# Loading a quarter of one weight piece by transfers of 8 partitions, on DMA engines 0 to 7 alone

## The chip, the cores and the metric

One core of one Trainium2 chip. The metric is the device time of one execution in microseconds, median of several.

## The reference

Two branches work on the same layer-normalised row block of four rows (batch 4, one position, D = 576), and their outputs are summed with the input: attention over the last 2048 positions of a cache (16 key/value heads, 32 query heads of 128), and a mixer with a gated MLP.

```
xn = layernorm(x)
h  = gelu(layernorm(xn) @ w1); hs = shift(h) @ w2; x1 = xn + hs
h2 = gelu(layernorm(x1) @ w3) @ w4            # w3: 576 x 4608, w4: 4608 x 576
out = x + attention(xn, k_cache, v_cache, wq, wo) + (x1 + h2)
```

The arithmetic is small. The weights and the cache windows, 88.5 MB in bfloat16, have to be read once.

## The kernel before

(A partition is one of the 128 rows of the on-chip memory, SBUF. A DMA engine is one of 16 units that move data between memories. A semaphore is a counter that engines raise and wait for.)

Every engine has a list of operations with sort keys; all loads but one small one are issued from one queue (SyncE), in the order wq, w2, w1, w3, K cache, V cache with wo in between, and w4 last. w4 comes in five pieces of 18, 9, 6, 2 and 1 rows per partition, so that little matmul work remains after the last one:

```python
W4_ROWS = (18, 9, 6, 2, 1)
...
for n, rc in enumerate(W4_ROWS):
    v = w4_t[:, len(w4tile) * D:(len(w4tile) + rc) * D]
    ev_w4.append(add_dma([(v, B_w4[base:base + 128 * rc, :].rearrange("(p r) n -> p (r n)", r=rc))], ("w4", n),
                         ["hT1", "hs1"] if n == 0 else [], KT + 5 + n))
    # ... (tiles of the piece are noted, base advances)
```

`add_dma` issues one transfer for each pair of destination and source and counts 16 semaphore increments for each. TensorE waits for a piece and accumulates it:

```python
for n, (t0, t1_) in enumerate(W4N):
    # f: for each tile t of the piece and each half h: ACC[h] += h2T[:, t]^T @ w4 tile
    if n < last_p:
        add("pe", f, waits=[ev_w4[n]], sig=f"MO{n}", key=KT + 20 + n)
    # else: one operation for each half, so that both halves can be copied and stored at once
```

A piece of `rc` rows is a transfer of 128 partitions with one contiguous run of `rc` x 1,152 bytes each: 20,736, 10,368, 6,912, 2,304 and 1,152 bytes. A tile `kt` of 32 KB per partition (transposed keys, then probabilities) is free after the middle of the kernel; the experiments use it as a target for additional loads.

## Time and profile before

| | before |
|---|---|
| median time | 216.02 us (215.91 to 217.14, 6 runs) |
| span of the profiled execution | 214.1 us |
| read from memory | 88.49 MB, 427 GB/s from 20 to 208 us |
| last landing of w4 | 211.47 us |

The page is read here by three things: the row of DMA share in the slices (which engine is full), the chain that ended last (what the end hangs on), and the stretches near the end. The prediction below shows these lines. Two more things come from the trace's own records rather than from a view: the time of each semaphore increment (16 for a transfer of 128 partitions, which I read as one for each DMA engine that finishes its part), and the start and duration of each packet. A packet here is one contiguous run: 10,368 bytes take 389 ns on one engine, 6,912 take 262, 2,304 take 93.

These are the one-microsecond stretches of the kernel before near its end. The columns are the stretch and its length, busy time of PE, PEld, DVE, ACT and POOL, the granted clock, the DMA share and GB/s:

```profile
206.00:207.00 1.00, 1.00 (x20) 0.72 (x18) 0.00 (x0) 0.00 (x0) 0.00 (x0) 1.00 0.92 387
207.00:208.00 1.00, 1.00 (x14) 0.48 (x10) 0.00 (x0) 0.00 (x0) 0.00 (x0) 1.00 1.02 430
208.00:209.00 1.00, 1.00 (x9) 0.36 (x8) 0.00 (x0) 0.00 (x0) 0.00 (x0) 1.00 0.98 400
209.00:210.00 1.00, 1.00 (x18) 0.55 (x14) 0.00 (x0) 0.00 (x0) 0.00 (x0) 1.00 0.76 289
210.00:211.00 1.00, 0.62 (x12) 0.41 (x12) 0.00 (x0) 0.00 (x0) 0.00 (x0) 1.00 0.44 165
```

The rate stays near 400 until 209 us and then falls with the DMA share: engines run out of work, those that still work keep their pace (289 GB/s at a share of 0.76, 165 at 0.44; packets of 2,304 bytes take 93 ns before 209 us and after). In such short stretches a long packet seems to be counted whole in one of them (a share goes up to 1.22 below), so a value may be off by some tens of GB/s.

### The profile page before, as it was taken

The numbers are of one execution on the slowest core, as the hardware profiler recorded it, in microseconds if no ns is written. First come the engines' busy times: TensorE is split into PE (matmuls) and PEld (weight loads), VectorE is DVE, ScalarE is ACT, GpSimd is POOL, SyncE is SP. The second block draws the span as 40 slices with busy tenths as digits, with TensorE's granted clock in tenths as the row PEclk, the third lists the DMA queues.
The fourth block names the chain that finished last, engine by engine and source line by source line (L and its number), as shares of the span: only waits on it lengthen the run. The fifth ranks groups of instructions, "written<-read, shape, count | busy, mean of one in ns | idle before, by whom it ended". The sixth has DMA issues, their size and how long they took to land. (4 is left out here: it accounts for less than half of the span.)

```text
span 214.1 us, 5906 instructions
## 1 busy us (share of the span) xinstructions
PE 145.6 (68%) x2642; PEld 108.9 (51%) x2646; DVE 76.5 (36%) x150; ACT 61.0 (29%) x75; POOL 10.9 (5%) x37
## 2 busy tenths in 40 slices
PE   0157787999999999999996178033444333336995
PEld 0023312888878887888774068033434333334542
DVE  5305400577676676666664830100010011001000
ACT  2001402466655665666666620000000000000000
POOL 8301000000001000000000000000000000000000
PEclk9999699999999999999999655555555555555799
DMA  7999999999999999999999999999999999999992
GB/s 282 404 385 445 441 407 438 419 427 416 435 429 429 422 435 429 424 426 435 429 426 426 429 429 425 419 432 429 429 422 429 435 429 419 430 436 426 428 409 104
DMA packets 7459, 88.66 MB, mean 414 GB/s; under 512 B 1292, under 2 KB 1688, under 8 KB 2456
## 3 DMA queue, kind: packets, MB, share of 16 engines
q1 hardware_dynamic: 7432, 88.50, 97.7%
q8 instruction: 8, 0.13, 0.2%
q14 instruction: 3, 0.02, 0.0%
q10 hardware_dynamic: 16, 0.01, 0.0%
HBM read 88.49 MB, written 0.00 MB: 413 GB/s over the span
## 5 line engine op out<-in xcount | busy, mean ns | idle before, releaser
L340 PE MATMUL ps<-perm_bf,ring 128*128 128x128 bf16 x1024 | 61.7, 220 | 0.6
L340 PEld LDWEIGHTS ps<-perm_bf,ring 128*128 128x128 bf16 x1024 | 57.5, 98 | 8.9 <-issue 8.6
L347 DVE COPY kt<-ps 128x1024 bf16<-128x1024 bf16 x80 | 52.3, 687 | 24.8 <-PE ps L340 24.3
L421 PE MATMUL ps<-PTpad,ring 128*128 128x8 bf16 x1024 | 29.7, 168 | 41.2 <-PEq L584 37.7
L346 ACT ACTIVATE kt<-ps 128x1024 bf16<-128x1024 bf16 x48 | 48.5, 1023 | 29.1 <-PE ps L340 28.3
L421 PEld LDWEIGHTS ps<-PTpad,ring 128*128 128x128 bf16 x1024 | 28.7, 104 | 42.3 <-issue 42.2
L561 ACT ACTIVATE out_sb<-ps 4x288 bf16<-4x288 f32 x1 | 0.4, 401 | 87.2 <-PE ps L438 87.2
L354 PE MATMUL ps<-kt,Qs 128*32 128x512 bf16 x272 | 17.8, 382 | 1.4 <-PEq L584 1.4
L410 DVE TENSOR_TENSOR PTpad<-PT,mU_bf 128x512 bf16<-128x512 bf16 x16 | 6.4, 420 | 29.7 <-PE ps L421 29.7
L433 DVE TENSOR_TENSOR OTn<-ps,rinvB 128x32 bf16<-128x32 f32 x4 | 0.8, 191 | 34.2 <-PE ps L421 34.2
L523 PE MATMUL ps<-w,x1nT 128*32 128x384 bf16 (+2 forms) x65 | 11.3, 766 | 0.8 <-DMA w<-in_B_w_dram 0.5
L354 PEld LDWEIGHTS ps<-kt,Qs 128*32 128x32 bf16 x272 | 5.8, 96 | 6.8 <-issue 1.5
L375 POOL COPY Qs<-Qpad 128x128 bf16<-128x128 bf16 x16 | 4.6, 293 | 87.0 <-PE ps L354 75.0
L301 PE MATMUL ps<-kt,xnT 128*32 128x512 bf16 x32 | 3.6, 631 | 4.3 <-DMA kt<-in_A_wq_dram 4.3
L523 PEld LDWEIGHTS ps<-w,x1nT 128*32 128x32 bf16 x65 | 3.3, 113 | 6.3 <-issue 3.9
L438 PE MATMUL ps<-w,ORT 128*4 128x288 bf16 x64 | 5.8, 357 | 0.4 <-DVE ORT L460 0.4
L278 PE MATMUL ps<-ident_bf,xn_bf 4*128 4x4 bf16 x8 | 0.6, 170 | 8.0 <-DVE ragsrc L271 8.0
L560 DVE CAST out_sb<-ps 4x288 bf16<-4x288 f32 x1 | 0.4, 446 | 14.5 <-PE ps L438 14.5
L438 PE MATMUL ps<-w,h2T_sb 128*4 128x288 bf16 x72 | 5.0, 286 | 0.4 <-DMA w<-in_B_w_dram 0.4
L392 PE MATMUL ps<-kt,permT_bf 128*128 128x512 bf16 x3 | 1.8, 608 | 4.9 <-DVE kt L391 4.8
L544 DVE COPY h2T_sb<-ps 128x16 bf16<-128x16 bf16 x1 | 0.2, 166 | 13.6 <-PE ps L538 13.6
L438 PEld LDWEIGHTS ps<-w,ORT 128*4 128x4 bf16 x64 | 3.3, 106 | 3.1 <-DVE ORT L460 1.0
(99 smaller groups left out, 61.6 us busy)
## 6 DMA issues: line engine op xcount, KB each, us to landing
ring<-in_A_k_cache_dram SPq DMA_DIRECT2D x32, 1024.0 KB, 13.0
ring<-in_A_v_cache_dram SPq DMA_DIRECT2D x32, 1024.0 KB, 15.1
w<-in_B_w_dram SPq DMA_DIRECT2D x2, 2304.0 KB, 22.9
w<-in_A_wo_dram SPq DMA_DIRECT2D x2, 2304.0 KB, 20.3
kt<-in_A_wq_dram SPq DMA_DIRECT2D x1, 4096.0 KB, 12.2
w<-in_B_w_dram SPq DMA_DIRECT2D x1, 2592.0 KB, 27.4
w<-in_B_w_dram SPq DMA_DIRECT2D x3, 576.0 KB, 14.5
w<-in_B_w_dram SPq DMA_DIRECT2D x1, 1296.0 KB, 30.0
```

The lines of the kernel that those rows point to most:

```text
L301: ins = e.matmul(Qps[k][32 * g:32 * g + 32, :], lhsT=x_, rhs=w, start=(r == 0), stop=(r == 4), tile_position=(0, 32 * g), skip_group_check ...
L340: ins = e.transpose(tb[n % 4][:, t, :], slot_t(c)[:, 8 * k + t, :], perm_bf[:])
L346: return "act", lambda e: e.activation(out=ktbuf[:, n % 16], in_=tb[n % 4], func=ACTF.Copy)
L347: return "dve", lambda e: e.tensor_copy(out=ktbuf[:, n % 16], in_=tb[n % 4])
L354: ins = e.matmul(Sps[32 * u:32 * u + 32, q, :].rearrange("p (t i) -> p t i", t=16), lhsT=Qs[:, c % NPOS, 32 * u:32 * u + 32], rhs=ktgrp[:, ...
L375: P(lambda e, c=c, cc=cc: e.tensor_copy(out=Qs[:, c % NPOS, :], in_=Qpad_t[:, 128 * cc:128 * cc + 128]), waits=["qT", "qs_zero"] + ([f"SC{ ...
L392: add("pe", lambda e, q=q: e.matmul(ps[:, 4 + q % 3, :], lhsT=permT_bf[:], rhs=PTx[:, q, :], start=True, stop=True), waits=[f"PTx{q}", "pe ...
L410: return lambda e: e.tensor_tensor(out=PTpad[:, c % 2], in0=PTv[:, :, cc, :].unsqueeze(2).to_broadcast([128, NT, NU, 2]), in1=mU_bf[:].uns ...
L421: ins = e.matmul(o_, lhsT=slot_t(c)[:, t, :], rhs=PTpad[:, c % 2, t].rearrange("p u e -> p (u e)"), start=(t == 0), stop=(t == NT - 1))
L433: add("dve", lambda e, hv=hv: e.tensor_tensor(out=hv(OTn), in0=OTps.rearrange("p (b h) -> p b h", b=B), in1=hv(rinvB), op=ALU.mult), waits ...
L438: return e.matmul(ACC[h], lhsT=lhsT, rhs=rhs, start=start, stop=stop, tile_position=(0, 32 * h), skip_group_check=True)
L523: ins = e.matmul(H2ps[k][32 * g:32 * g + 32, 128 * off:128 * (off + cnt)].rearrange("p (c x) -> p c x", c=cnt), lhsT=x_, rhs=w.rearrange(" ...
```

## The change

At the end eight of the 16 DMA engines finish after the other eight. The change is meant to shift a little work: of the second piece, three quarters of the partitions (p mod 4 = 0, 1, 2) are loaded by transfers of 32 partitions, which all 16 engines share, and the last quarter (p mod 4 = 3) by four transfers of 8 partitions, which engines 0 to 7 carry alone. Engines 0 to 7 then carry 10 rows of this piece and engines 8 to 15 carry 6, instead of 8 each.

The packet records carry no engine number, so these numbers are names: 0 to 7 are the eight engines that carry a transfer of 8 partitions.

```diff
+LOW8 = 1
 W4_ROWS = (18, 9, 6, 2, 1)
...
             v = w4_t[:, len(w4tile) * D:(len(w4tile) + rc) * D]
-            ev_w4.append(add_dma([(v, B_w4[base:base + 128 * rc, :].rearrange("(p r) n -> p (r n)", r=rc))], ("w4", n),
+            w4_src = B_w4[base:base + 128 * rc, :].rearrange("(p r) n -> p (r n)", r=rc)
+            rows = [slice(0, 128)] if n != LOW8 else [slice(a, 128, 4) for a in range(3)] + [slice(3 + a, 32 + a, 4) for a in range(0, 128, 32)]
+            ev_w4.append(add_dma([(v[a], w4_src[a]) for a in rows], ("w4", n),
                                  ["hT1", "hs1"] if n == 0 else [], KT + 5 + n))
```

## The prediction

> **What bounds the kernel now.** I began with the slices of the page: if one row is full over the whole span, that row is the bound.
>
> ```profile
> PE   0157787999999999999996178033444333336995
> DMA  7999999999999999999999999999999999999992
> GB/s 282 404 385 445 441 407 438 419 427 416 435 429 429 422 435 429 424 426 435 429 426 426 429 429 425 419 432 429 429 422 429 435 429 419 430 436 426 428 409 104
> ...
> HBM read 88.49 MB, written 0.00 MB: 413 GB/s over the span
> ```
>
> DMA is the only row at 9 from the second slice to the last but one; PE sits at 3 or 4 for a third of the span. The kernel is a stream of 88.49 MB at some 427 GB/s, and no compute engine sets its time. The chain that ended last says where the end hangs:
>
> ```profile
> by line: DMA w<-in_B_w_dram 14.6%; SPq L177 1.2%; PE ps L421 0.9%; PE ps L438 0.6%; issue 0.3%; DVE out_sb L560 0.2%
> ...
> 179.19 31.22 DMA w<-in_B_w_dram
> 210.41 0.04 issue
> 210.46 1.39 PE ps L438 x18
> 211.85 0.44 DVE out_sb L560
> ```
>
> From 179 to 210 us the end waits for w4, then for 18 short matmuls, a cast and the store. The timeline of the end shows that PE follows each piece as it lands:
>
> ```profile
> 205.32 2.37 PE L438 MATMUL ps<-w,h2T_sb 128*4 128x288 bf16 x36
> 207.62 1.25 PE L444 MATMUL ps<-zeros_bf 128*128 128x512 bf16 x5
> 208.81 1.27 PE L438 MATMUL ps<-w,h2T_sb 128*4 128x288 bf16 x18
> 210.46 1.35 PE L438 MATMUL ps<-w,h2T_sb 128*4 128x288 bf16 x18 [0.38 <-DMA w<-in_B_w_dram]
> 211.51 0.08 PEld L438 LDWEIGHTS ps<-w,h2T_sb 128*4 128x4 bf16 x2 [0.23 <-DMA w<-in_B_w_dram]
> ```
>
> The last line is the key: the last weight loads still wait 0.23 us for a DMA, so the last landing sets the end. After it come about 2.6 us of fixed tail. Stretches show that the DMA engines do not all stop together:
>
> ```profile
> 20.00:208.00 188.00, 135.54 (x2533) 104.19 (x2538) 69.46 (x128) 58.36 (x70) 3.81 (x13) 0.77 1.01 427
> 208.00:212.00 4.00, 3.42 (x41) 1.57 (x38) 0.16 (x1) 0.13 (x1) 0.00 (x0) 1.00 0.54 214
> ```
>
> The last two columns are DMA share and GB/s. Before 208 us the 16 engines are full; afterwards only part of them works.
>
> The trace's semaphore records give each engine's landing. The 16 increments of the last w4 piece come at 209.54 to 210.45 us (eight), then, after a gap, at 210.97 to 211.47 (eight). Early on the spread is small: 24.03 to 24.46 us for the second piece of w3. So eight engines are late at the end, and the kernel ends with the latest of them. Why they are late: another queue carries a few big packets.
>
> ```profile
> q8 instruction: 8, 0.13, 0.2%
> ```
>
> Each has 16,384 bytes and takes 1.01 to 1.10 us. Packet records carry no engine number, but a packet starts about 4 ns before the end of the one before it on its engine, so I chained them into 16 lanes. Seven lanes stall once by 1.00 to 1.08 us, each at the end of one of the first seven such packets (27.4, 41.5, 49.6, 118.7, 127.6, 133.9, 159.1 us); an eighth lane is late by about as much from 47 us on, without a record that explains it. These eight lanes are the late ones. The eighth packet, at 209.0 us, meets the lane that had led.
>
> [...]
>
> **The change part by part.** The second piece has 128 rows of 10,368 bytes (1,296 KB), 8 rows per engine, median 389 ns a packet: 3.11 us per engine.
> - *Moved:* three transfers of 32 partitions give every engine 3 x 2 = 6 rows. Four transfers of 8 partitions give engines 0 to 7 four more. So 0 to 7 carry 10 rows and 8 to 15 carry 6: plus and minus 2 x 0.389 = 0.78 us. Bytes are unchanged.
> - *Added in the stream:* one semaphore packet per transfer and engine. One costs about 10 ns between data packets, and the next packet 5 ns (267 against 262 ns). Engines 0 to 7 have six more, about 0.09 us; 8 to 15 two more, 0.03 us.
> - *Added on the issuing queue:* six more issues at about 0.44 us (median of the w rows) put the last issue near 183 us instead of 180.5. Nothing of w4 lands before 197 us: hidden.
> - *PE, DVE, ACT:* the instruction order is the same. The piece's wait moves to a full count of 112.
>
> If 8 to 15 are the late ones, the late group's last landing goes from 211.47 to 211.47 - 0.78 + 0.03 = 210.72, the early group's from 210.45 to 210.45 + 0.78 + 0.09 = 211.32. The maximum falls by 0.15 us. PE keeps up: the third piece lands by about 210.25 instead of 210.41, so the matmuls ahead of the last also move up. On 215.94 this gives 215.79, and I say **215.8 us**. The means favour this reading: the groups lie about 1.2 us apart, and the change moves 1.56 us of difference between them, so it overshoots somewhat. More could not be gained than the distance from the last engine to the mean, some 0.9 us.
>
> **The rivals.**
> - *The late group is not 8 to 15.* If it is 0 to 7, or mixed, a late engine gets the rows: 211.47 + 0.87 = 212.34, and the kernel takes 216.8. Against it: [...]that eight and only eight engines are late. I give this 15%.
> - [...]Half of the small transfers write partitions 64 to 127[...]. [...]each such row takes twice as long: 2 x 0.39 = 0.78 us more for each of the two. Then the early group ends near 212.1 and the late near 211.5: some 0.6 us slower, 216.5. [...]Against it: no packet of the piece before is over 396 ns, and the cache loads with every second partition run as fast as the rest, 427 GB/s, though they too are not whole 128-partition transfers. About 35%.
> - *Hidden anyway.* The second piece is not what the end waits for; if each engine's queue weren't in order, its shift would vanish. The spread between lanes is carried through all the last pieces unchanged, which speaks against it. It would give 215.9.
> - *The stalls differ between executions.* Then the balance gained in one is lost in another; the runs of 215.93, 215.94 and 216.82 show such a spread.
>
> **Range and chances.** About half the weight lies at 215.7 to 215.9, a third around 216.4, the rest near 216.8. The range 215.2 to 217.0 holds these and the noise of runs. 2% is 4.3 us, beyond every case: faster 0.01, same 0.98, slower 0.01.
>
> **What would show it.** The last piece's 16 landings: right if all lie within about 1.2 us and end near 211.3, in one group or with the order reversed; the rival of identity if the spread grows to some 2.7 us. [...]The DMA share in 208 to 212 us should stay near 0.54. The slices should remain as they are, and the last w4 issue near 183 us. The prediction is wrong if a transfer of 8 partitions uses other engines, or if strided rows are cut into smaller packets.

## The result and the profile after

| | before | after |
|---|---|---|
| median time | 216.02 us (215.91 to 217.14, 6 runs) | 218.13 us (217.94 to 218.82, 6 runs) |
| ratio, 95% interval | | 1.0089 (1.0062 to 1.0115) |
| span of the profiled execution | 214.1 us | 216.3 us |
| last landing of w4 | 211.47 us | 213.66 us |

A ratio here and below is the mean time of one kernel's fast runs over that of the other's of the same rounds, so it is not quite the ratio of the medians. Where I give a difference in us, it is (ratio - 1) x 216: here +1.9 us. The kernel became slower, outside the predicted range of 215.2 to 217.0; the change stays below 2%, which the prediction called "same" and gave 0.98.

The chain that ended last, after:

```profile
by line: DMA w<-in_B_w_dram 13.5%; SPq L178 3.0%; PE ps L424 0.9%; PE ps L441 0.6%; issue 0.5%; DVE out_sb L563 0.2%
...
183.30 29.30 DMA w<-in_B_w_dram
212.60 0.04 issue
212.64 1.39 PE ps L441 x18
214.03 0.43 DVE out_sb L563
```

The chain has the same form, and everything in it stands 2.2 us later from the third piece on: 212.60 us where the kernel before had 210.41. The tail behind it is as long as before. The timeline of the end shows where the first delay is met:

```profile
207.63 1.25 PE L447 MATMUL ps<-zeros_bf 128*128 128x512 bf16 x5
210.84 0.95 PEld L441 LDWEIGHTS ps<-w,h2T_sb 128*4 128x4 bf16 x18 [2.46 <-DMA w<-in_B_w_dram]
210.84 1.27 PE L441 MATMUL ps<-w,h2T_sb 128*4 128x288 bf16 x18 [1.96 <-DMA w<-in_B_w_dram]
212.64 1.35 PE L441 MATMUL ps<-w,h2T_sb 128*4 128x288 bf16 x18 [0.53 <-DMA w<-in_B_w_dram]
```

The changed piece itself is late: its matmuls start at 210.84 instead of 208.81 us. The first piece still starts at 205.32 us in both, so all of the loss arises between. The same stretches of the end as before:

```profile
206.00:207.00 1.00, 1.00 (x20) 0.74 (x18) 0.00 (x0) 0.00 (x0) 0.00 (x0) 1.00 1.22 346
207.00:208.00 1.00, 1.00 (x14) 0.48 (x10) 0.00 (x0) 0.00 (x0) 0.00 (x0) 1.00 0.80 194
208.00:209.00 1.00, 0.88 (x5) 0.20 (x2) 0.00 (x0) 0.00 (x0) 0.00 (x0) 1.00 1.07 253
209.00:210.00 1.00, 0.00 (x0) 0.00 (x0) 0.00 (x0) 0.00 (x0) 0.00 (x0) 1.00 1.03 245
210.00:211.00 1.00, 0.16 (x4) 0.13 (x6) 0.00 (x0) 0.00 (x0) 0.00 (x0) 1.00 0.80 285
```

This is the reading that matters. From 207 to 210 us the DMA share is about as full as ever, and yet the rate is 194 to 253 GB/s instead of 430 and 400: every engine has a packet under way, and the packets take nearly twice as long. A busy engine is not an engine at full rate. The packet records say the same: of the second piece's 128 packets 33 take over 400 ns (up to 776; before: none, 396 at most), and of the third piece's, which the change does not touch, 91 of 128 take over 280 ns (median 434; before: 262). The 16 landings of the last piece spread over 2.9 us (210.76 to 213.66). The prediction had set a spread of some 2.7 us as the sign that a late engine gets the rows; slow packets spread the landings too, so the sign doesn't tell the two apart.

The issuing queue is not the cause. It is busy for longer, but ends well before the data is needed:

```profile
177.89 6.92 SPq L178 DMA_DIRECT2D w<-in_B_w_dram  x11
```

The last issue ends at 184.8 us, and the first piece starts on the engines at 196.6 us.

### The profile page after: what moved, and what is told of

Read it like the earlier page. It is cut to its first block, busy times and chain, and to the rows that moved or that the text cites.

```text
span 216.3 us, 5912 instructions
## 1 busy us (share of the span) xinstructions
PE 145.3 (67%) x2642; PEld 108.8 (50%) x2646; DVE 76.2 (35%) x150; ACT 61.1 (28%) x75; POOL 11.0 (5%) x37
## 2 busy tenths in 40 slices
DMA packets 7523, 88.66 MB, mean 410 GB/s; under 512 B 1356, under 2 KB 1752, under 8 KB 2520
## 5 line engine op out<-in xcount | busy, mean ns | idle before, releaser
L441 PEld LDWEIGHTS ps<-w,h2T_sb 128*4 128x4 bf16 x72 | 2.9, 84 | 5.2 <-DMA w<-in_B_w_dram 4.2
```

What stands on the lines that cost most here:

```text
L441: return e.matmul(ACC[h], lhsT=lhsT, rhs=rhs, start=start, stop=stop, tile_position=(0, 32 * h), skip_group_check=True)
```

## The experiments

**Theory.** Two of the four small transfers make engines 0 to 7 write partitions 67 to 127. If other engines are writing there at the time, both wait. Which engine writes which partitions of a transfer of 128, no trace names; that each has partitions of its own was my assumption. The experiments test it by the destination alone. What I call the own partitions of engines 0 to 7 is what made no packet slow: row by row 3, 7, ..., 31 and 35, 39, ..., 63 (extra_low: 0 of 272 packets; tag: none). Into 67, 71, ..., 127 it was 132 of 272 (extra_high); these I call others' partitions. **Rivals:** strided or small transfers are slow in themselves; a transfer on 8 engines is slow; the source rows collide; or the loss is just the uneven load. In the expectations, what the theory lets one expect comes first, then the rival.

In the following, a packet counts as slow over 400 ns (10,368 bytes) or 280 ns (6,912 bytes), and of two counts the first is for 10,368 bytes.

### split32: the split without the small transfers

```diff
-            rows = ... + [slice(3 + a, 32 + a, 4) for a in range(0, 128, 32)]
+            rows = [slice(0, 128)] if n != LOW8 else [slice(a, 128, 4) for a in range(4)]
```

> One part of the change alone: the second w4 piece in four transfers of 32 partitions, none of 8. [...]each engine keeps its 8 rows, no row meets another engine, all packets of 10,368 bytes stay at 389 to 396 ns, time within 0.3 us of before (216.0). Rival (splitting into strided transfers itself costs, whatever engines carry them): 0.5 us or more slower, packets over 400 ns.

Measured: 216.07 us, ratio 0.9995 (0.9979 to 1.0012), no slow packet. Strided destinations, more transfers and more semaphores cost nothing that can be seen. The loss comes from the four small transfers.

### sixteen: engines even, partitions not

```diff
+            rows = ... [slice(a, 128, 4) for a in range(3)] + [slice(3, 64, 4), slice(67, 128, 4)]
```

> The last quarter as two transfers of 16 partitions (3 to 63, then 67 to 127) instead of four of 8: every one of the 16 engines carries 8 rows, so the engines are balanced as before, but all 16 write into one half of the partitions at a time. [...]slow packets (600 to 780 ns) as in the changed kernel, 0.8 to 2.5 us slower than before. Rival (the transfers on 8 engines are what is slow, or the overload of engines 0 to 7): no slow packet, 216.0 to 216.3.

Measured: 217.05 us, ratio 1.0048 (1.0031 to 1.0064), +1.0 us; 57 and 68 slow packets in the two pieces, the longest at 679 ns. Its stretches:

```profile
206.00:207.00 1.00, 1.00 (x20) 0.71 (x18) 0.00 (x0) 0.00 (x0) 0.00 (x0) 1.00 0.96 301
207.00:208.00 1.00, 1.00 (x16) 0.51 (x11) 0.00 (x0) 0.00 (x0) 0.00 (x0) 1.00 1.01 318
```

If 16 rows go to 16 engines (an estimate: the changed kernel's transfers of 8 rows have 8 semaphore packets, those of 32 have 16), all engines carry the same load, and the stream still falls to some 310 GB/s. So neither the uneven load nor the count of 8 engines is needed for the effect: two transfers of 16 rows, each into one half of the partitions, are enough.

### extra_low and extra_high: the same load and source, two destinations

The kernel before, with two redundant transfers of 8 partitions behind the second piece, into the free tile `kt` (the result does not use them):

```diff
+EXTRA = [(slice(3 + a, 32 + a, 4), 0, slice(3 + a, 32 + a, 4)) for a in (0, 32)]    # extra_low
+EXTRA = [(slice(67 + a, 96 + a, 4), 0, slice(3 + a, 32 + a, 4)) for a in (0, 32)]   # extra_high
...
+        x_src = B_w4[2304:3456, :].rearrange("(p r) n -> p (r n)", r=9)
+        ev_extra = add_dma([(kt_t[d, c:c + 5184], x_src[s_]) for d, c, s_ in EXTRA], "extra", ["PTy3"], KT + 6.5)
+        add("sp", lambda e: None, [ev_extra], None, 10002)
```

> Kernel before, plus two redundant transfers of 8 partitions into free space, both into partitions 0 to 63: engines 0 to 7 carry 2 rows more, as in the change, but into the partitions that they write anyway. [...]all packets at 389 to 396 ns; engines 0 to 7 end 0.8 us later, so between +0.0 (if they are the early ones) and +0.85 us (if some are late). Rival (8-partition transfers are slow in themselves): packets of 600 ns and more, about half of the change's loss or all of it, +1 to +2 us.

> The same two redundant transfers from the same source rows, but into partitions 64 to 127[...]. [...]slow packets of 10,368 and 6,912 bytes, DMA rate down to about 250 GB/s for 2 to 4 us, +1.5 to +3 us. Rival (8-partition transfers slow in themselves, or the source rows): the same as the run into partitions 0 to 63.

| | time, us | ratio | slow packets, 10,368 / 6,912 bytes | last landing |
|---|---|---|---|---|
| extra_low | 216.66 | 1.0034 (1.0018 to 1.0051) | 0 of 144 / 0 of 128 | 211.96 |
| extra_high | 218.62 | 1.0110 (1.0090 to 1.0129) | 45 of 144 / 87 of 128 | 213.83 |

The stretches of extra_low, then of extra_high:

```profile
207.00:208.00 1.00, 1.00 (x18) 0.58 (x14) 0.00 (x0) 0.00 (x0) 0.00 (x0) 1.00 0.99 414
208.00:209.00 1.00, 1.00 (x7) 0.40 (x5) 0.00 (x0) 0.00 (x0) 0.00 (x0) 1.00 0.97 403
```

```profile
207.00:208.00 1.00, 1.00 (x16) 0.53 (x11) 0.00 (x0) 0.00 (x0) 0.00 (x0) 1.00 0.99 249
208.00:209.00 1.00, 0.94 (x5) 0.21 (x3) 0.00 (x0) 0.00 (x0) 0.00 (x0) 1.00 0.89 228
```

This is the cleanest pair. Same number of engines, same rows read, same size and place in the queue; the destination partitions alone differ. Into partitions 3 to 63: 414 and 403 GB/s (430 and 400 before). Into 67 to 127: 249 and 228 GB/s. The destination costs 1.0110 - 1.0034 = 0.0076, 1.6 us. The uneven load by itself costs 0.7 us, which suggests that some of engines 0 to 7 were among the late ones.

One other thing is mixed into this time. In the trace of extra_high the granted TensorE clock (the third number from the right) falls before the last matmuls:

```profile
212.00:213.00 1.00, 0.19 (x2) 0.09 (x4) 0.00 (x0) 0.00 (x0) 0.00 (x0) 0.66 0.50 189
213.00:214.00 1.00, 1.00 (x12) 0.55 (x10) 0.00 (x0) 0.00 (x0) 0.00 (x0) 0.50 0.06 21
```

The last 18 matmuls take 2.32 us instead of 1.35, and the tail behind the last landing is 3.59 us instead of 2.62. The traces of low8_0 (3.50) and chunks (3.70) below show the same, those of before, the change, extra_low, sixteen and shift1 do not. What the destination does to the stream is therefore read more safely from rates and landings: in these two traces (by chance the slowest and the fastest of their four executions) the last landing is 1.87 us later. Why the clock falls, and in how many of the executions, the record does not show.

### shift1: the same half, but the neighbour's partitions

```diff
+EXTRA = [(slice(7 + a, 36 + a, 4), 0, slice(3 + a, 32 + a, 4)) for a in (0, 32)]
```

> Kernel before, plus two redundant transfers of 8 partitions from the same source rows, into partitions 7, 11, ..., 35 and 39, ..., 67: mostly the lower half, but by row number each engine would write its neighbour's partitions. If the rule is one writer per group of partitions: slow packets and +1 us or more. If what counts is crossing between the lower and the upper half, or if the engine follows the partition's address: nearly as the run into the engines' own partitions (no or few slow packets, +0.7 us).

Measured: 218.03 us, ratio 1.0095 (1.0059 to 1.0131), +2.1 us; 40 and 62 slow packets. The stretches:

```profile
207.00:208.00 1.00, 1.00 (x16) 0.51 (x11) 0.00 (x0) 0.00 (x0) 0.00 (x0) 1.00 1.10 301
208.00:209.00 1.00, 0.98 (x5) 0.25 (x3) 0.00 (x0) 0.00 (x0) 0.00 (x0) 1.00 0.93 292
```

Crossing from one half to the other is not needed: of these 16 rows one alone, into partition 67, leaves the lower half. Each row goes here where mostly the next row went in extra_low, and that is enough. It also speaks for engines going by row number in a transfer of 8 partitions: if they followed the partition's address, shift1 would differ from extra_low in one row alone, the one into partition 67 instead of 3.

### pair: how far a crowded pair of partitions reaches

```diff
+EXTRA = [(slice(67, 100, 32), c, slice(67, 100, 32)) for c in (0, 5184)]
```

> Kernel before, plus two redundant transfers of only 2 partitions (67 and 99), 41 KB in all[...]. Local theory (only engines that write into the same group of partitions wait for each other): at most three engines slow, DMA rate no lower than about 370 GB/s, at most some ten slow packets of 6,912 bytes, end +0 to +1.6 us. Spreading theory (one crowded group holds up engines that write elsewhere): more than three engines slow, rate well below 370 GB/s for a while.

Measured: 216.86 us, ratio 1.0019 (0.9997 to 1.0042): the time is unclear, the trace is not. Four rows, 41 KB, make 23 and 47 slow packets, the longest of 10,368 bytes at 1,271 ns. The stretches:

```profile
206.00:207.00 1.00, 1.00 (x22) 0.73 (x18) 0.00 (x0) 0.00 (x0) 0.00 (x0) 1.00 1.10 439
207.00:208.00 1.00, 1.00 (x18) 0.57 (x14) 0.00 (x0) 0.00 (x0) 0.00 (x0) 1.00 0.98 290
208.00:209.00 1.00, 1.00 (x7) 0.41 (x5) 0.00 (x0) 0.00 (x0) 0.00 (x0) 1.00 0.92 348
```

Two engines carry these rows; if only they and one that writes there otherwise were slow (three is the theory's count, not the trace's), and even if they stood still, the other 13 would move 13/16 of 427 = 347 GB/s. The rate over 207 to 208 us is 290, and sampled in steps of 0.3 us from the packet records it is 308, 308 and 314 from 207.3 to 208.2 us. The count of packets says it without any rate: three engines carry only 3 x 8 = 24 packets of 6,912 bytes, and 47 are slow. So engines beyond these three are held up too. By which path it spreads, no run here shows.

### Sizes: low8_0, low8_2, low8_3 and one_high

The change on another piece (`LOW8 = 0`, `2` or `3`), and extra_high with one transfer instead of two (`EXTRA = [(slice(67, 96, 4), 0, slice(3, 32, 4))]`).

> The change on the first w4 piece instead of the second: rows of 20,736 bytes, twice as long. Theory (loss grows with the bytes written into others' partitions): rate near 250 GB/s for about twice as long as in the changed kernel, loss about 4 us, less what engines 0 to 7 make good. Rival (a fixed cost for each 8-partition transfer): +2 us as in the changed kernel.

> The change on the third piece, rows of 6,912 bytes, between the changed kernel (10,368: +1.9 us) and the fourth piece (2,304: no slow packet, no loss). In proportion to the bytes: +1.2 us. With a part absorbed, as 20,736 (+5.3), 10,368 (+1.9) and 2,304 (0) bytes suggest: +0.3 to +0.9 us.

> The change on the fourth piece: rows of 2,304 bytes, less than a quarter as long. Theory of loss by bytes: +0.3 to +0.7 us, with slow packets only among the last two pieces. Rival of a fixed cost: +2 us.

> One redundant transfer of 8 partitions into 64 to 127 instead of two: 10,368 bytes per engine written into another engine's partitions. If a short backlog is absorbed: no or few slow packets, +0.4 us. If the loss is in proportion to the bytes: about half of the loss of the two (2.4 us), +1.0 to +1.4 us, with a rate near 250 GB/s for 1.5 to 2.5 us.

| run | bytes that each of engines 0 to 7 writes into others' partitions | ratio | us |
|---|---|---|---|
| low8_3 | 2 x 2,304 = 4,608 | 0.9990 (0.9968 to 1.0011) | -0.2 |
| one_high | 10,368 | 1.0048 (1.0029 to 1.0066) | +1.0 |
| low8_2 | 2 x 6,912 = 13,824 | 1.0067 (1.0050 to 1.0084) | +1.4 |
| the change | 2 x 10,368 = 20,736 | 1.0089 (1.0062 to 1.0115) | +1.9 |
| low8_0 | 2 x 20,736 = 41,472 | 1.0248 (1.0213 to 1.0283) | +5.4 |

The loss grows with the bytes, about 0.1 us for each KB that an engine writes into others' partitions, and it is not a fixed cost for each transfer. The load of engines 0 to 7 grows along with the bytes and is not taken off (0.7 us in extra_low). With 4.6 KB nothing is seen, not even a slow packet of the 2,304 bytes. For low8_0 I had expected about 4 us: in its trace the last landing is 4.3 us later than before, and another 0.9 us is the longer tail at the lower clock. For low8_2 the reading with a part absorbed (0.3 to 0.9 us) falls; the one in proportion (1.2 us) is near. The one 10 KB transfer of one_high already shows slow packets (41 and 85), so little is absorbed; its rate, 298 to 321 GB/s from 206 to 209 us, did not fall to the expected 250. Why 4.6 KB cost nothing is not settled: it may be that at that place, near the end, some engines are already idle.

### chunks: the same bytes in shorter packets

```diff
+ each transfer of 8 partitions cut into four: (v[a, c:c + 1296], w4_src[a, c:c + 1296]) for c in (0, 1296, 2592, 3888)
```

> The change, with each transfer of 8 partitions cut into four of 2,592 bytes per row: the same bytes, as many into others' partitions, but packets as short as in the fourth piece, which showed no slow ones. If the backlog of bytes counts: +1.5 to +2.5 us as in the changed kernel. If the length of a packet counts: no slow packets, within 0.8 us of before.

Measured: 219.91 us (218.50 to 221.39), ratio 1.0186 (1.0126 to 1.0246), +4.0 us, twice the loss of the change and more than either expectation. 84 of the 128 short packets are over 108 ns (104 is the shortest, 170 the median). So short packets are no way out; what spared the fourth piece is not that its packets are short. They look worse than long ones, but not by the whole 2 us: in the traced executions the last landing is 3.0 us later than before (the change: 2.2), and 1.1 us is the longer tail at the lower clock. The rest stays open; the 12 additional transfers with their semaphore packets are a rival that no run separates.

### tag: which engines are late

Three redundant transfers of 8, 4 and 2 partitions, each row meant for its engine's own partitions, so that the number of additional rows names the engine:

```diff
+EXTRA = [(slice(3, 32, 4), 0, slice(3, 32, 4)), (slice(2, 15, 4), 0, slice(3, 16, 4)), (slice(1, 6, 4), 0, slice(3, 8, 4))]
```

> Kernel before, plus redundant transfers of 8, 4 and 2 partitions, each row into the partitions that its engine writes anyway. No packet should be slow. The number of additional rows (3 for engines 0 and 1, 2 for 2 and 3, 1 for 4 to 7, none for 8 to 15) marks the lanes, and so tells which engines are late at the end. The prediction's step (late = 8 to 15): every marked lane is early. If five of 8 to 15 and three of 0 to 7 are late, as the run with two more rows in the own partitions suggests, three marked lanes are late, and time is +0.3 to +1.2 us.

One execution, 216.16 us; no slow packet. I chained the packets into 16 lanes, as in the prediction, and took the start of the first w4 piece in each lane, before anything of the additional rows, in us:

```
engines 0, 1     (3 rows more): 196.85  197.44
engines 2, 3     (2 rows more): 196.72  197.87
engines 4 to 7   (1 row more):  196.95  197.38 | 198.38  198.43
engines 8 to 15  (none):        196.58  196.76  197.10 | 198.31  198.36  198.56  198.72  198.74
```

Right of the bar are the late lanes: two of 4 to 7 and five of 8 to 15. The late group is not 8 to 15. Two lanes carry a row of each of the three transfers, two carry two rows and four carry one; beyond that the trace does not name the engines one by one. In extra_low three of engines 0 to 7 are late and five of 8 to 15. These are two other executions than the one that the prediction read; whether the same engines are late in each is not shown.

## Why the prediction was wrong

- **What bounds the kernel, the landings, the 0.78 us per two rows, the tail:** right. Two rows more in an engine's own partitions were two packets of 389 to 394 ns in extra_low; the tail behind the last landing stayed at about 2.6 us in the changed kernel.
- **Issue and semaphores:** right in effect. The last issue ended at 184.8 us rather than near 183, and was hidden; split32 shows 0.9995.
- **Failed step, the sum itself:** "the early group's from 210.45 to 210.45 + 0.78 + 0.09 = 211.32" takes each moved row at 0.39 us wherever it is written. In the changed kernel the piece's packets, those of the small transfers among them, ran at 389 to 398 ns only until about 206.2 us and at up to 776 ns afterwards. The destination alone costs about 1.6 us (extra_high against extra_low), 1.87 us by the landings of the two traces.
- **The rival that came true, mis-sized:** rows of engines 0 to 7 meeting other engines in partitions 64 to 127, at about 35%, put the loss at some 0.6 us: two rows of each engine taking twice as long, which was an estimate of mine. Slow packets came, of up to 776 ns where 396 had been the longest. The size counted only the two engines that meet. The measured stream falls to about half as a whole for some 3.7 us, and pair shows further engines held up as well (47 slow packets of 6,912 bytes, and three engines carry 24 in all). Sampled in steps of 0.3 us, the rate goes down to 223 GB/s here, 215 in extra_high and 212 in low8_0; a stream held to eight lanes' full rate would be 8 x 26.7 = 213 GB/s (an estimate from 10,368 bytes in 389 ns). The lowest rates are near it, but no run shows such a limit by itself. What I set against it was weak: that no packet before was over 396 ns says nothing of small transfers, which the kernel before does not have for w4, and I took the cache loads with 64 partitions as evidence although the trace does not say which engine writes which of their partitions.
- **Failed step, which engines are late:** the identity 8 to 15 was an estimate of mine that no trace showed, and it does not hold: tag has two of 4 to 7 among the seven late ones. Even without any crowding, two more rows on engines 0 to 7 cost 0.7 us in extra_low (which takes none from 8 to 15), as my first rival said in kind, with 15%. The reading of the stalls was too small as well: after each of the seven packets of 16,384 bytes the next packet of that lane takes 0.45 to 0.55 us longer than its like, so each of the seven costs a lane some 1.5 us and not 1.00 to 1.08, and the two groups of landings lie 1.4 us apart by their means and not 1.2. Three further delays have no such packet on record: a lane is idle for 0.3 us, and then a packet takes 989 to 1,265 ns (from 46.6, 89.1 and 182.8 us on). So these packets do not account for all of the lateness.
- **Range:** it ended at 217.0 because I took the two rivals one by one, and the second at too small a size. Both came true together.
- **Not tested:** the rival that the stalls differ between executions.

What the change set out to do can't be done this way: a row that engine 0 takes over still goes to the partition it went to before, and rows from engines 0 to 7 into 67 to 127 cost 1.6 us by their destination (extra_high against extra_low). No version tried beats the kernel before. That the destination makes the loss is shown by extra_low, extra_high and shift1; sixteen agrees. That two engines meet in the same partitions is the reading that fits all four; no trace shows the meeting itself. How it spreads to further engines, and what short packets add, is open.

## What to carry to other kernels

Balance the destination partitions as well as the DMA engines: here small transfers into partitions other than their engines' own nearly halved the whole stream (from some 427 to 194 to 253 GB/s) at a full DMA share. Read the DMA share together with GB/s and packet durations; full and slow at once came here with packets of up to 776 ns instead of 389. Look at the clock of the last stretches before you put all of a time down to the loads. Before shifting work from late engines to early ones, mark which engines are late by a harmless additional load, and ask what the receiving engine will write to.
